# TensorE streams the identity into unused columns of the products' PSUM bank

## The chip, the cores and the metric

The kernel runs on one core of a Trainium2 chip. The metric is the device time of one execution in microseconds (us). Smaller is better.

## The reference

Attention with a top-k mask feeds a feed-forward block with squared ReLU.

```python
# q, k, v: (8, 8, 576, 64) f32; w_in: (512, 2048); w_out: (2048, 512)
scores = scale * q @ k^T                        # per batch and head, 576 x 576
kth = np.partition(scores, -32, axis=-1)[..., -32:-31]
scores = np.where(scores >= kth, scores, -1e9)  # keep each row's 32 largest
scores = scores - scores.max(-1, keepdims=True)
attn = np.exp(scores) / (np.exp(scores).sum(-1, keepdims=True) + 1e-9)
x = (attn @ v).transpose(0, 2, 1, 3).reshape(4608, 512)
h = np.maximum(x @ w_in, 0.0)
out = h * h @ w_out
```

## The kernel before

The attention is cut into 144 steps (`U = 144`). A step `u` handles two blocks of 128 rows of scores, each 576 wide. The steps are software-pipelined, and the instruction order on each engine is written out by hand (`pin` keeps it). In the main loop, while VectorE searches the 32 largest of step `u`, TensorE makes the scores of `u + 1`, and ScalarE, GpSimd and the DMA queues carry the weights of earlier steps on.

One step on the four engines, in the names of the profile:

- **Scores.** `scores(u + 1)` (L319) fills two PSUM banks, `sc_a` with the first halves of the rows and `sc_b` with the second. `sc_a` may be written once VectorE's `most` (L352) of the step before has read it. `sc_b` may be written once VectorE's two operations on `cats` (L376, L377) have read what it held. Between `sc_a` and `sc_b` TensorE does what `in_gap` holds: the ten products of an older step's weights with the values (`weigh`, L570, into the bank `av_ps`), the transposes of finished tokens (L648, L666) and of the coming pair's q and k (L202).
- **Copies.** ScalarE copies both halves to the tile `s` (L329: `s<-sc_a`, then `s<-sc_b`). Then VectorE forms `most` from `sc_a` and the copied second half.
- **Search.** VectorE runs four rounds of `MAX8` and `MATCH_REPLACE8` (L443, L445, L451). Its place for `most` of the next step is between the third and the fourth round.
- **Weights.** ScalarE makes the exponentials (L526), a DMA transposes them to `wT` (L535), `weigh` sums them with the values, VectorE inverts the row sums (L586, L591) and ScalarE's `place` scales the result into `x_tok` or `x_rem` (L610, L615).
- **Dense block.** After the scores TensorE runs pieces of the feed-forward block: `up` (L695, sixteen matmuls of 128 columns) and `down` (L765, four of 512 columns). Where no piece is ready, `idle_piece` (L786) streams the identity into the bank `dn_ps`. From step 123 on, a written table (`PLAN`) says which pieces run; in that stretch `carry_far` (L392) also moves a part of `most` back into `sc_b` on TensorE in some steps.

The bank `av_ps` holds three steps' products of 2 x 65 columns each, so 390 of its 512 columns are used.

Of the kernel before, what the change touches and what calls it, by code (L numbers as in the profile page):

```python
# [13 lines left out]
f32 = mybir.dt.float32  # L14
# [9 lines left out]
def kernel(  # L24
# [9 lines left out]
    nc = tc.nc  # L34
# [53 lines left out]

    flags = const.tile([128, 6, 8 * 4 * 9], bf16, name="flags")
    cats = const.tile([128, 2, 2, WIDE], f32, name="cats")  # L90
    av = ps_one.tile([128, 3, 2, 65], f32, name="av_ps")


    pairs = [(b, pr) for b in range(B) for pr in range(H // 2)]
# [2 lines left out]

    fetches = []
    after_far, next_far = [], []

    def by_head(t):
        return t.rearrange("p (a d) -> p a d", a=2)
# [77 lines left out]
    def prep_units(i):  # L180
        q_raw, k_raw, v_raw = raw[i]
        qkT = heads.tile([128, 512 + 640], f32, name="qkT")
        qT, kT = qkT[:, 0:512], qkT[:, 512:1152]
        k_rest = kT.rearrange("p (n d) -> p n d", d=64)[:, 0:10:9]
        bd, va = qbd[i % 5], vau[i % 8]
        prep[i] = (qT, kT, bd, va)

        def twice(t):
            return t.rearrange("p (o d) -> p o d", o=1).broadcast_to([128, 2, 64])

        def main(which, src):
            bank = []

            def turn_chunks(some):
                if not bank:
                    bank.append(ps_one.tile([128, 512], f32, name="gen", bufs=2))
                for c in some:
                    if side_by_side(i):
                        pin(nc.tensor.transpose(bank[0][:, c * 128:(c + 1) * 128], src[:, c * 128:(c + 1) * 128], id_f[:, :]))
                        continue  # L200
                    for a in range(2):
                        pin(nc.tensor.matmul(out=bank[0][64 * a:64 * a + 64, c * 128:(c + 1) * 128], lhsT=src[:, a * 256 + c * 64:a * 256 + (c + 1) * 64],  # L202
                                             rhs=id_f[:, :], start=True, stop=True))

            def go():
                turn_chunks((2, 3) if bank else range(4))
                pin(nc.scalar.activation((qT, kT[:, 64:576])[which], bank[0][:, :], AF.Copy, scale=(scale, 1.0)[which]))
                next_far.append(lambda: last_values(which))
            go.ahead = lambda: turn_chunks((0, 1))
            return go  # L210


        def first_step():
            for j, bank in ((0, "gen"), (1, "gen"), (2, "dn_ps"), (3, "sc_a")):
                if bank == "sc_a":
                    tp = ps_sc.tile([128, 2, 512], f32, name=bank)[:, 0, :]
                else:
                    tp = ps_one.tile([128, 512], f32, name=bank, bufs=2 if bank == "gen" else None)
                if j < 2:
                    for c in range(2):  # L220
                        pin(nc.tensor.transpose(tp[:, c * 128:(c + 1) * 128], k_raw[:, 2 * j + c], id_f[:, :]))
                    to, got = kT[:, 64 + j * 256:64 + (j + 1) * 256], tp[:, 0:256]
                elif j == 2:
                    pin(nc.tensor.transpose(tp[:, 0:128], q_raw[:, 0], id_f[:, :]))
                    to, got = qT[:, 0:128], tp[:, 0:128]
                else:
                    pin(nc.tensor.transpose(tp[:, 0:64], k_raw[0:64, 4], id_f[0:64, 0:64]))
                    to, got = k_rest, twice(tp[:, 0:64])
                if j % 2:
                    pin(nc.vector.tensor_copy(to, got))  # L230
                else:
                    pin(nc.scalar.activation(to, got, AF.Copy, scale=scale if j == 2 else 1.0))

        def first_q():
            tp = ps_one.tile([128, 512], f32, name="gen", bufs=2)
            for c in range(1, 4):
                pin(nc.tensor.transpose(tp[:, c * 128:(c + 1) * 128], q_raw[:, c], id_f[:, :]))
            pin(nc.scalar.activation(qT[:, 128:512], tp[:, 128:512], AF.Copy, scale=scale))

        def rest(both=(0, 1)):  # L240
            tp = ps_one.tile([128, 512], f32, name="gen", bufs=2)
            for which in both:
                src = (q_raw, k_raw)[which]
                last = src[0:64, 512:640] if i else src[0:64, 4]
                pin(nc.tensor.transpose(tp[:, which * 64:(which + 1) * 64], last, id_f[0:64, 0:64]))
            if 0 in both:
                pin(nc.scalar.activation(bd[0:64, 0:64], tp[0:64, 0:64], AF.Copy, scale=scale))
                pin(nc.scalar.activation(bd[64:128, 64:128], tp[64:128, 0:64], AF.Copy, scale=scale))
            if 1 in both:
                pin(nc.scalar.activation(k_rest, twice(tp[:, 64:128]), AF.Copy))  # L250

        def last_values(x):
            assert i < 8 or av_left[i - 8] == 0
            half = slice(64 * x, 64 * x + 64)
            pin(nc.scalar.activation(va[half, 4 + x, :, 0:64], by_head(v_raw[half, 512:640]), AF.Copy))

        def values():
            assert i < 8 or av_left[i - 8] == 0
            pin(nc.scalar.activation(va[:, 0:4, :, 0:64], v_raw[:, 0:512].rearrange("p (a c d) -> p c a d", a=2, c=4), AF.Copy))

        def all_values():
            values()
            last_values(0)
            last_values(1)

        if i == 0:
            return [first_step, first_q, all_values, lambda: rest((0,))]
        return [main(0, q_raw), main(1, k_raw), rest, values]
# [37 lines left out]
    def scores(u, between=None):  # L306
        ps = [ps_sc.tile([128, 2, 512], f32, name=f"sc_{j}") for j in "ab"]
        js = (1, 0) if u < 2 else (0, 1)

        def half(j):  # L310
            for x, (i, c, a) in enumerate(steps[u]):
                qT, kT, bd, va = prep[i]
                k0 = j * HALF + 64 * (1 - x)
                if c < 4:
                    r = slice(64 * a, 64 * a + 64)
                    lhsT, rhs = qT[r, c * 128:(c + 1) * 128], kT[r, k0:k0 + HALF]
                else:
                    lhsT, rhs = bd[:, :], kT[:, k0:k0 + HALF]
                pin(nc.tensor.matmul(out=ps[j][:, x, 0:HALF], lhsT=lhsT, rhs=rhs, start=True, stop=True))  # L319

        half(js[0])
        if not between:
            half(js[1])
        two_s = scores_of[u // 2 % 3]
        s = two_s[:, u % 2]
        st[u] = {"s": s, "ps": ps, "both_s": two_s}
        st[u]["cat"] = cats[:, u % 2]
        for j in js:
            pin(nc.scalar.activation(s[:, :, j * HALF:(j + 1) * HALF], ps[j][:, :, 0:HALF], AF.Copy, scale=sign(u)))  # L329
            if u == 0 and j == 1:  # L330
                pairs_of(0)
                soon.pop(0)()
            if between and j == js[0]:
                between()
                half(js[1])
        for i, c, a in steps[u]:
            qk_left[i] -= 1
# [291 lines left out]
    def x_unit(now, b, c):  # L629
# [12 lines left out]
        def by_tensor():  # L642
            if late:
                tp = bank(2, [128, 2 * KH, 128], bf16)[:, 0:KH]
            else:
                tp = ps_one.tile([128, KH, 128], bf16, name="gen", bufs=2)[:, :, :]
            for kh in range(KH):
                pin(nc.tensor.transpose(tp[:, kh, :], x_tok[b, c][:, kh * 128:(kh + 1) * 128], id_h[:, :]))  # L648

            def rest():  # L650
                if late:
                    pin(nc.vector.tensor_copy(to, tp))
                else:
                    pin(nc.scalar.activation(to, tp, AF.Copy))  # L654
                if late or at_step[0] >= U - 2:
                    done()
                else:
                    fresh.append(done)
            return rest
# [18 lines left out]
    def block(xt, stores):  # L678
# [3 lines left out]

        def up(f0):
            def go():
                if f0 == 0:
                    held["h2"] = ffp.tile([128, NF, 128], bf16, name="h2", bufs=5)
                if tail:
# [70 lines left out]

        def down(c, part):
            def go():  # L760
                if part == 0:
                    held["op"] = ps_one.tile([128, 512], f32, name="dn_ps")
                op = held["op"]
# [17 lines left out]
        ups.extend(up(f) for f in range(0, NF, per))  # L781

    def idle_piece():
        hp = ps_one.tile([128, 512], f32, name="dn_ps")
        for kh in range(KH):
            pin(nc.tensor.matmul(out=hp[:, :].rearrange("p (o n) -> p o n", o=4), lhsT=id_h[:, :], rhs=id_h[:, :].rearrange("p (o n) -> p o n", o=1).broadcast_to([128, 4, 128]),  # L786
# [180 lines left out]
    for u in range(U):  # L967
# [94 lines left out]
            turn_x(u)  # L1062
        if u < U - 2:
            dense(u, 1)
        load_weights(1 if u else 2)

    assert len(ups) == 2 and not downs and len(behind) == 1 and not fresh and not moves and not soon_moves
# [217 lines left out]
```

## Time and profile before

| | |
|---|---|
| median of 3 runs | 852.09 us (849.92 to 852.37) |
| profiled execution, its own time | 850.69 us |
| its span, first to last instruction | 848.9 us |
| mean granted TensorE clock | 0.982 of 2.4 GHz |
| VectorE (DVE) busy | 811.6 us, 96% |
| ScalarE (ACT) busy | 759.0 us, 89% |
| GpSimd (POOL) busy | 741.4 us, 87% |
| TensorE (PE) busy | 687.5 us, 81% |

The profile comes from one execution. A busy share is an average over the start, the long middle (about 20 to 690 us), the stretch in which `PLAN` rules (about 690 to 826 us) and the end. TensorE's matmuls overlap, so two that follow each other at full rate start closer together than one lasts. The granted clock is given as a share: 1.00 is 2.4 GHz and 0.50 is 1.2 GHz.

### The profile page before, as it was taken

The numbers are of one execution on the slowest core, as the hardware profiler recorded it, in microseconds if no ns is written. First come the engines' busy times: TensorE is split into PE (matmuls) and PEld (weight loads), VectorE is DVE, ScalarE is ACT, GpSimd is POOL, SyncE is SP. The second block draws the span as 40 slices with busy tenths as digits, with TensorE's granted clock in tenths as the row PEclk, the third lists the DMA queues.
The fourth block names the chain that finished last, engine by engine and source line by source line (L and its number), as shares of the span: only waits on it lengthen the run. The fifth ranks groups of instructions, "written<-read, shape, count | busy, mean of one in ns | idle before, by whom it ended". The sixth has DMA issues, their size and how long they took to land.

```text
span 848.9 us, 21844 instructions
## 1 busy us (share of the span) xinstructions
PE 687.5 (81%) x6901; PEld 434.4 (51%) x6992; DVE 811.6 (96%) x3697; ACT 759.0 (89%) x1699; POOL 741.4 (87%) x781
## 2 busy tenths in 40 slices
PE   7678887887788788777888778787888788888986
PEld 3334345554555555455555555555555554556555
DVE  5999999999999999999999999999999999989993
ACT  4677779999999999999999999999999999989894
POOL 8998988988889889999889989898889997988982
PEclk9999999999999999999999999999999989999999
DMA  8889999999999999999999999999999998677862
GB/s 174 161 138 212 206 206 182 200 206 228 205 203 210 214 224 200 208 212 209 227 195 201 215 213 216 206 214 215 223 199 227 226 204 194 171 155 165 184 149 56
DMA packets 247371, 166.61 MB, mean 196 GB/s; under 512 B 200016, under 2 KB 224848, under 8 KB 247248
## 3 DMA queue, kind: packets, MB, share of 16 engines
q1 hardware_dynamic: 224544, 80.32, 54.2%
q0 software_dynamic: 21488, 84.42, 41.2%
q8 instruction: 57, 0.93, 0.5%
q14 instruction: 66, 0.54, 0.2%
q10 hardware_dynamic: 1216, 0.39, 0.2%
HBM read 37.75 MB, written 9.44 MB: 56 GB/s over the span
## 4 chain that ended last, share of the span: by engine, by line
DVE 53%; ACT 21%; PE 13%; issue 6%; DMA 3%; POOL 2%; SPq 0%; ACTq 0%; POOLq 0%; DVEq 0%
DVE m L445 14%; DVE cats L451 13%; DVE cats L443 8%; DVE most L352 8%; PE sc_a L319 5%; DVE cats L445 4%; DVE cats L376 4%; ACT rl L702 3%; DVE cats L377 3%; ACT w_two_b L526 2%; ACT w_two_c L526 2%; ACT w_two_a L526 2%; ACT sc_b L383 2%; ACT s_c L329 1%; PE sc_b L319 1%
## 5 line engine op out<-in xcount | busy, mean ns | idle before, releaser
L445 DVE MAX8 m<-cats 128x8 f32<-128x116 f32 (+3 forms) x864 | 259.9, 342 | 0.0
L410 POOL TENSOR_TENSOR cats<-cats,most 128x576 int32<-128x576 int32 (+1 forms) x144 | 230.3, 1599 | 3.2 <-DVE most L352 1.0
L695 PEld LDWEIGHTS <-w_in 128*128 128x128 bf16 x2304 | 142.7, 100 | 38.7 <-issue 16.7
L451 DVE MATCH_REPLACE8 cats<-m,cats 128x116 f32<-128x116 f32 (+1 forms) x576 | 157.7, 281 | 0.0
L319 PE MATMUL sc_b<-qkT 64*128 64x288 f32 x512 | 100.4, 466 | 62.8 <-DVE cats L377 56.2
L695 PE MATMUL gen<-xT,w_in 128*128 128x128 bf16 x2016 | 136.7, 224 | 4.1 <-ACT xT L654 3.3
L765 PE MATMUL dn_ps<-w_out,h 128*128 128x512 bf16 x456 | 125.5, 389 | 12.0 <-issue 8.5
L319 PE MATMUL sc_a<-qkT 64*128 64x288 f32 x512 | 98.0, 459 | 41.5 <-DVE most L352 38.2
L443 DVE MAX8 cats<-cats 128x8 f32<-128x288 f32 (+1 forms) x288 | 113.2, 434 | 0.0
L712 ACT ACTIVATE h<-rl 128x512 bf16<-128x512 f32 x136 | 85.7, 630 | 4.3
L702 ACT ACTIVATE rl<-gen 128x512 f32<-128x512 f32 x142 | 83.5, 588 | 3.2 <-PE gen L695 2.7
L401 POOL TENSOR_TENSOR cats<-s_c 128x576 int32<-128x576 int32 (+1 forms) x48 | 66.4, 1383 | 21.0 <-ACT s_c L329 19.3
L319 PEld LDWEIGHTS sc_b<-qkT 64*128 64x128 f32 x512 | 41.6, 190 | 82.5 <-PE av_ps L570 34.1
L570 PEld LDWEIGHTS <-wT 128*128 128x128 bf16 (+1 forms) x1600 | 54.8, 100 | 56.2 <-issue 46.8
L401 POOL TENSOR_TENSOR cats<-s_a 128x576 int32<-128x576 int32 (+1 forms) x48 | 65.2, 1357 | 20.2 <-ACT s_a L329 17.1
L401 POOL TENSOR_TENSOR cats<-s_b 128x576 int32<-128x576 int32 (+1 forms) x48 | 65.2, 1358 | 17.1 <-ACT s_b L329 14.8
L319 PEld LDWEIGHTS sc_a<-qkT 64*128 64x128 f32 x512 | 40.0, 188 | 74.0 <-DVE most L352 49.2
L383 ACT ACTIVATE sc_b<-most 128x288 f32<-128x288 f32 x136 | 57.1, 420 | 22.6 <-DVE most L352 19.0
L765 PEld LDWEIGHTS <-h 128*128 128x128 bf16 x544 | 45.4, 99 | 59.3 <-issue 22.5
L451 DVE MATCH_REPLACE8 cats<-cats 128x96 f32<-128x96 f32 x288 | 67.4, 241 | 0.0
L376 DVE TENSOR_TENSOR cats<-sc_b,most 128x288 f32<-128x288 f32 x144 | 63.1, 438 | 1.7 <-ACT sc_b L383 1.7
L377 DVE TENSOR_TENSOR cats<-sc_b,most 128x288 f32<-128x288 f32 x144 | 64.2, 446 | 0.0
(243 smaller groups left out, 1682.8 us busy)
## 6 DMA issues: line engine op xcount, KB each, us to landing
s_a<-gone_b POOLq DMA_DIRECT2D x9, 1152.0 KB, 7.8
s_b<-gone_a POOLq DMA_DIRECT2D x9, 1152.0 KB, 8.0
s_c<-gone_b POOLq DMA_DIRECT2D x9, 1152.0 KB, 7.6
s_a<-gone_a POOLq DMA_DIRECT2D x9, 1152.0 KB, 7.8
s_b<-gone_b POOLq DMA_DIRECT2D x9, 1152.0 KB, 7.7
s_c<-gone_a POOLq DMA_DIRECT2D x8, 1152.0 KB, 7.8
v_raw<-in_v_dram SPq DMA_DIRECT2D x64, 128.0 KB, 3.5
k_raw<-in_k_dram SPq DMA_DIRECT2D x63, 128.0 KB, 3.5
```

Source lines behind the costliest of these rows:

```text
L319: pin(nc.tensor.matmul(out=ps[j][:, x, 0:HALF], lhsT=lhsT, rhs=rhs, start=True, stop=True))
L376: pin(tt(in_two(cat[:, :, QUADS:NEXT]), far, near, op=ALU.max))
L377: pin(tt(in_two(cat[:, :, SMALL:QUADS]), far, near, op=ALU.min))
L401: pin(tt(less, s[:, :, 0:wide].bitcast(i32), s[:, :, HALF:HALF + wide].bitcast(i32), op=ALU.add))
L410: pin(tt(less, less, d["most"][:, :, 0:wide].bitcast(i32), op=ALU.subtract))
L443: pin(nc.vector.max(out=cat[:, x, NEXT:TOPS], in_=cat[:, x, 0:searched]))
L445: pin(nc.vector.max(out=m[r][:, x, :], in_=part(r, x)))
L451: pin(nc.vector.match_replace(out=part(r, x), in_to_replace=m[r][:, x, :], in_values=part(r, x), imm_value=NEG))
L695: pin(nc.tensor.matmul(out=hp[:, n * n_rows:(n + 1) * n_rows], lhsT=w_in[:, kh, (f0 + n) * 128:(f0 + n + 1) * 128], rhs=xt(kh), start=(kh ...
L702: pin(nc.scalar.activation(kept["rl"][:, :], hp, AF.Relu))
L712: pin(nc.scalar.activation(h2, flat, AF.Square))
L765: pin(nc.tensor.matmul(out=op[:, :], lhsT=held["h2"][:, f, c * 128:(c + 1) * 128], rhs=w_out[:, f, :], start=(f == 0), stop=(f == NF - 1)))
```

## The change

The tile of the products' bank becomes all 512 columns wide; the products keep columns 0 to 389. A new function `keep_warm(n)` gives TensorE `n` matmuls that stream 122 columns of the identity into columns 390 to 511, which nothing reads. It is called in two places, from step 8 on: eight matmuls in `scores`, behind what `in_gap` holds and ahead of the second half of the scores; and up to eight at the end of a step, behind its dense pieces, if the work counted in `pe_work` (a rough sum of the step's transposes and dense pieces in us) is under 2.4.

```diff
-    av = ps_one.tile([128, 3, 2, 65], f32, name="av_ps")
+    av_bank = ps_one.tile([128, 512], f32, name="av_ps")
+    av = av_bank[:, 0:390].rearrange("p (t x d) -> p t x d", t=3, x=2)
...
+    pe_work = [0.0]
+
+    def keep_warm(n):
+        for _ in range(n):
+            pin(nc.tensor.matmul(out=av_bank[:, 390:512], lhsT=id_h[:, :], rhs=id_h[:, 0:122], start=True, stop=True))
...
             def turn_chunks(some):
...
+                pe_work[0] += 0.11 * len(some)
...
             if between and j == js[0]:
                 between()
+                if u >= 8:
+                    keep_warm(8)
                 half(js[1])
...
+            pe_work[0] += 0.3
...
+                pe_work[0] += 0.9
...
+                pe_work[0] += 0.86
...
+        pe_work[0] += 0.86
...
         if u < U - 2:
             dense(u, 1)
+            if u >= 8 and pe_work[0] < 2.4:
+                keep_warm(min(8, int((2.4 - pe_work[0]) / 0.055)))
+            pe_work[0] = 0.0
```

In the program this gives 1682 new matmuls, each with its own weight load: 136 groups of eight ahead of the second half of the scores, and 98 groups of two to eight at step ends. The order on VectorE, ScalarE, GpSimd and SyncE, and what their instructions wait for, stays as it was.

On TensorE, in the step whose scores have the number 137 (in the stretch that `PLAN` rules), the piece before ends the ten products (`av_ps<-vau_g`) and goes on to `sc_b`:

```order
L570 LDWEIGHTS wT
L570 MATMUL av_ps<-vau_g,wT 128x65
L319 MATMUL sc_b<-qkT 128x288 [waits DVE_49,PE_49]
L319 MATMUL sc_b<-qkT 128x288
L695 LDWEIGHTS w_in
```

In the changed kernel the same place (its lines are counted eight to twelve further on) reads:

```order
L580 LDWEIGHTS wT
L580 MATMUL av_ps<-vau_g,wT 128x65
L106 LDWEIGHTS id_h
L106 MATMUL av_ps<-id_h 128x122
...
L106 LDWEIGHTS id_h
L106 MATMUL av_ps<-id_h 128x122
L327 MATMUL sc_b<-qkT 128x288 [waits DVE_49,PE_49]
L327 MATMUL sc_b<-qkT 128x288
L707 LDWEIGHTS w_in
```

Eight pairs of a weight load and a matmul now stand between the last product and `sc_b`, in front of the wait of `sc_b`; they wait for nothing themselves.

On TensorE at a step end in the middle of the run (the dense piece of step 71, then the scores of 72), the piece before is:

```order
L765 LDWEIGHTS h_5841
L765 MATMUL dn_ps<-w_out,h_5841 128x512
L319 MATMUL sc_a<-qkT 128x288 [waits DVE_49]
L319 MATMUL sc_a<-qkT 128x288
L570 LDWEIGHTS wT [waits DMAHW5_49]
L570 MATMUL av_ps<-vau_g,wT 128x65 [waits Activation_49]
```

And in the changed kernel:

```order
L778 LDWEIGHTS h_6629
L778 MATMUL dn_ps<-w_out,h_6629 128x512
L106 LDWEIGHTS id_h
L106 MATMUL av_ps<-id_h 128x122 [waits Activation_49]
...
L327 MATMUL sc_a<-qkT 128x288 [waits DVE_49]
L327 MATMUL sc_a<-qkT 128x288
L580 LDWEIGHTS wT [waits DMAHW5_49]
L580 MATMUL av_ps<-vau_g,wT 128x65
```

The wait for ScalarE (for `place`, which reads the bank) has moved from the first product, behind `sc_a`, to the first new matmul, ahead of `sc_a`. That is so in 97 of the 98 groups at step ends.

## Rows read from the trace of the kernel before

**Rows 1.** Windows of the middle and the late stretch: start:end, length, busy by engine.

```profile
20.00:690.00 670.00, 541.37 (x5467) 338.21 (x5535) 665.57 (x3047) 615.50 (x1387) 602.61 (x594) 0.99 1.03 207
690.00:826.00 136.00, 117.75 (x1198) 77.35 (x1211) 125.86 (x580) 123.12 (x270) 116.25 (x117) 0.96 0.77 172
```

**Rows 2.** Timeline of a middle step, all engines: start, length, engine, line, operation [idle before].

```profile
402.20 0.76 PE L319 MATMUL sc_b<-qkT 64*128 64x288 f32 x4 [0.28 <-DVE cats L377]
...
403.86 0.64 ACT L329 ACTIVATE s_c<-sc_b 128x576 f32<-128x576 f32 x1
...
404.75 0.74 DVE L352 SCALAR_TENSOR_TENSOR most<-s_c,sc_a 128x576 f32<-128x576 f32 x1
404.87 0.53 ACT L610 ACTIVATE x_tok<-av_ps,rthree 128x64 bf16<-128x64 f32 x2
...
405.55 0.76 PE L319 MATMUL sc_a<-qkT 64*128 64x288 f32 x4 [0.18 <-DVE most L352]
```

**Rows 3.** Timeline of a late step, scores number 123, all engines.

```profile
694.22 0.76 PE L319 MATMUL sc_b<-qkT 64*128 64x288 f32 x4
...
695.02 0.65 ACT L329 ACTIVATE s_b<-sc_b 128x576 f32<-128x576 f32 x1
695.71 0.75 DVE L352 SCALAR_TENSOR_TENSOR most<-s_b,sc_a 128x576 f32<-128x576 f32 x1 [0.21 <-ACT s_b L329]
```

**Rows 4.** The same two ends of a late step, scores number 142.

```profile
811.74 0.76 PE L319 MATMUL sc_b<-qkT 64*128 64x288 f32 x4
...
813.23 0.76 DVE L350 TENSOR_TENSOR most<-sc_a,s_c 128x576 f32<-128x576 f32 x1
```

**Rows 5.** The same two of scores number 136.

```profile
776.08 0.76 PE L319 MATMUL sc_b<-qkT 64*128 64x288 f32 x4
...
777.70 0.76 DVE L352 SCALAR_TENSOR_TENSOR most<-s_c,sc_a 128x576 f32<-128x576 f32 x1 [0.34 <-ACT s_c L329]
```

**Rows 6.** The same two in a middle step, scores number 40.

```profile
232.44 0.65 PE L319 MATMUL sc_b<-qkT,qbd_e 128*128 128x288 f32 x2
...
233.81 0.75 DVE L352 SCALAR_TENSOR_TENSOR most<-s_c,sc_a 128x576 f32<-128x576 f32 x1
```

**Rows 7.** TensorE's timeline, up pieces and waits, 742 to 830 us.

```profile
752.14 0.76 PE L392 MATMUL sc_b<-most,id_f 128*128 128x144 f32 x4 [1.97 <-DVE most L352]
...
754.00 1.91 PE L695 MATMUL gen<-xT,w_in 128*128 128x128 bf16 x16
...
764.23 1.95 PE L695 MATMUL gen<-xT,w_in 128*128 128x128 bf16 x32
...
769.21 1.06 PE L695 MATMUL gen<-xT,w_in 128*128 128x128 bf16 x16
```

**Rows 8.** TensorE's timeline, 686 to 732 us.

```profile
693.60 0.46 PE L570 MATMUL av_ps<-vau_b,wT 128*128 128x65 bf16 x10 [1.85 <-DVE m L445]
...
718.17 0.48 PE L570 MATMUL av_ps<-vau_c,wT 128*128 128x65 bf16 x10 [1.37 <-DMA wT<-w_two_b]
...
719.21 1.33 PE L319 MATMUL sc_b<-qkT 64*128 64x288 f32 x4
```

**Rows 9.** Windows, columns as in rows 1; the eighth figure is the granted clock.

```profile
319.70:323.10 3.40, 3.06 (x14) 1.53 (x16) 3.40 (x19) 3.16 (x8) 3.13 (x4) 0.50 1.09 281
...
695.20:698.60 3.40, 3.30 (x32) 2.92 (x30) 2.36 (x9) 2.35 (x7) 2.84 (x3) 0.50 0.30 68
719.00:722.40 3.40, 3.40 (x27) 2.11 (x22) 2.92 (x15) 2.21 (x6) 2.42 (x3) 0.51 0.92 227
753.20:756.60 3.40, 3.40 (x23) 2.40 (x21) 2.56 (x15) 2.23 (x5) 3.21 (x5) 0.50 0.76 187
```

**Rows 10.** ScalarE's timeline, 688 to 706 us.

```profile
696.72 0.60 ACT L207 ACTIVATE qkT<-gen 128x512 f32<-128x512 f32 x1 [1.05 <-PE gen L202]
```

**Rows 11.** All engines, 755 to 758 us.

```profile
757.40 0.17 DVE L591 RECIPROCAL rsum<-av_ps 128x2 f32<-128x2 f32 x1 [1.64 <-PE av_ps L570]
```

**Rows 12.** ScalarE's waits from 20 to 690 us: total us, times, longest.

```profile
ACT sc_b L383 <- DVE most L352: 18.0, 47, 0.8
```

## The prediction

> **What bounds the kernel now.** I read the windows first, to see which engine is full in which stretch. From 20 to 690 us VectorE is busy 665.6 of 670.0 us [rows 1]: it stands still for 4.4 us in all, and a change on TensorE can win no more than that there. From 690 to 826 us it is busy 125.9 of 136.0 [rows 1]: 10 us of standing still, and TensorE, at 117.8 busy, is the engine to look at.
>
> The timeline then shows how far TensorE's scores are ahead of their use. In a middle step `sc_b` ends at 402.20 + 0.76 = 402.96; ScalarE comes to copy it only at 403.86, and the copy ends 0.25 us before `most` starts at 404.75 [rows 2]. So `sc_b` has 0.90 us until ScalarE comes, and VectorE another 0.25: a delay of half a us would not reach VectorE. In a late step it is otherwise: `sc_b` ends at 694.98, the copy starts 0.04 later, `most` starts 0.04 after the copy, and VectorE has waited for it [rows 3]. From the end of `sc_b` to `most` this takes 0.73 us, the copy and two hand-overs. At 811.74 it is 0.73 again [rows 4]. Stepping through the late stretch I find nine of its 21 steps like this, at 694.2, 702.6, 719.2, 726.4, 757.3, 763.2, 782.1, 787.9 and 811.7 (rows 3 are the first, rows 4 the last). There every delay of `sc_b` is a delay of VectorE.
>
> The last view is the clock. Its mean over the run is 0.982, and the loss sits in eight short stretches at 0.50, which is 1.2 GHz; four are in the middle, four from 681 us on. In the one at 319.7 VectorE is busy for all 3.40 us: half speed on TensorE costs nothing there. In the three at 695.2, 719.0 and 753.2 it is busy 2.36, 2.92 and 2.56 us [rows 9].
>
> **What the change adds: the matmuls.** Nothing is removed. In the timeline 32 matmuls of 128 columns take 1.95 us and 16 take 1.06 [rows 7], so one more costs 0.89 / 16 = 0.056 us; one of 122 columns costs about that. Eight are 0.45 us. At half clock 16 take 1.91 [rows 7], another 0.053 each, and eight are 0.87. All 1682 are 94 us of TensorE time, which has room only where TensorE waits.
>
> **Ahead of `sc_b`.** All 136 groups stand behind the products and in front of the wait of `sc_b`. Where TensorE waits for VectorE there by more than 0.45 us, the group is free. I went through the 136 places, taking the gap between TensorE's last work and `sc_b`: 59 of them are shorter than the group. What that costs goes by the slack behind `sc_b`.
> - The nine tight late steps pay in full: 9 x 0.45 = 4.05. The one at 719.2 is at half clock [rows 9], which adds 0.87 - 0.45 = 0.42. Together 4.5.
> - Four more late steps have a little slack. At 776.08 `sc_b` ends at 776.84 and `most` starts 0.86 later, 0.13 more than the tight 0.73 [rows 5]; this step pays 0.32. The other three have between 0.14 and 0.45. Together 0.9.
> - In the middle only three steps are as tight. The one at 232.44 ends at 233.09 with `most` 0.72 later [rows 6], so it and its twin at 431 pay 0.45 each, and one at 648 pays 0.3. Together 1.2.
>
> These delays add up, since each late step's chain starts from the `most` of the step before: TensorE waits for `most` at 752.14 [rows 7], then does its dense piece, `sc_a`, the products and `sc_b` in a row.
>
> **At step ends.** Of the 98 groups, 97 now wait for ScalarE's `place` ahead of `sc_a`. In the step of rows 2 `x_tok` ends at 405.40; four matmuls then end at 405.63, where `sc_a` had started at 405.55 [rows 2]. So `sc_a` comes about 0.1 us later; over the groups I find 0 to 0.6. What is queued behind it is `sc_a` and the products, and whoever waits for those has more than a us. It counts only where `sc_b` is pushed in turn, in two steps near 325 and 331: 0.6 us together, as an estimate.
>
> That it waits at all is what the Trainium skill says against the change (PSUM — Partial Sum Buffer, "PSUM bank collisions raise a hardware error"): a matmul and a reader are to be kept apart by bank and quadrant, and other columns of the bank don't help. By that rule the free columns spare no wait; the order of the changed kernel agrees, with 97 waits, and the sum without them would be 0.6 lower.
>
> **What the clock gives back.** The three late stretches cost VectorE at most the following. At 695.2 ScalarE waits 1.05 us for transposes at half clock [rows 10]; half of it goes at full clock, 0.5. At 719.21 `sc_b` takes 1.33 instead of 0.76 [rows 3, 8], 0.6, and what follows some 0.4 more. At 753.2 VectorE waits 1.64 us for the products [rows 11] behind sixteen matmuls that took 1.91 for 1.06: 1.6 with the others there. Together 3.1 us, and nothing in the middle. But what TensorE did before each fall was to wait: 1.85 us ahead of the products at 693.60, 1.37 us for a transposed `wT` at 718.17 [rows 8], 1.97 us for `most` at 752.14 [rows 7]. The new groups stand behind the first two of these waits in the queue, and ahead of the third only by a step, so they don't fill them. I count one of the three: 1.0 us. Bounds: 0 and 3.1.
>
> The Trainium skill (TensorE: Matmul & The Clock Gate, "Why this matters for your kernels") has the opposite rule: keep TensorE busy between its bursts, and the throttle stays away. The falls behind waits agree with it; by it the credit would be 3.1 instead of 1.0.
>
> **The sum.** 4.5 + 0.9 + 1.2 + 0.6 - 1.0 = 6.2 us slower. The profiled execution took 850.7 us, 1.4 below the median of the three runs; the four lie around 851.3. Added to the first this is 856.9, to the middle of the four 857.5. I say 857.0.
>
> **The unknown in the middle.** `sc_b` comes later in 48 of the 114 middle steps in which ScalarE would already be there, so ScalarE would stand still some 14 us more there (my estimate, 0.3 us each). ScalarE is busy 615.5 of 670 [rows 1], and 18.0 us of its rest are waits for `most` [rows 12], which shrink as it gets later. That cover takes in all 14, if it lies in the right steps. If a third of it doesn't, VectorE waits up to 5 us more. Between 0 and 5 I take 0, because the middle step of rows 2 has 0.25 us for VectorE on top.
>
> **Rivals.**
> 1. *The clock pays (faster).* All three late stretches go, and the groups lie in time that TensorE would have waited. Then 851.3 - 3.1 = 848.2. For it: the clock of the late stretch, 0.96 [rows 1], and that falls follow waits. Against it: the groups cost 0.45 us in nine steps where TensorE waits for nothing. It decides from the point at which a group delays the tight steps by less than 0.2 us on average. Chance 0.09.
> 2. *No change.* The delays are real but vanish at later waits for something else: the wait of 1.37 us for a `wT` [rows 8] shows that a DMA can end last. Half of the 5.4 late us lost that way, the middle costs absorbed too and two clock stretches gone: 851.3 + 2.7 - 2 = 852. That also covers the case in which the clock stays as it is and the groups are hidden. Chance 0.24.
> 3. *ScalarE becomes the bound of the middle.* The cover of 18.0 us doesn't fit, and the waits for `place` hold TensorE up when ScalarE is late. 857 + 5 = 862. For it: ScalarE's load; against: the slack of most middle steps. Chance 0.15.
>
> The forecast keeps 0.52.
>
> **How the numbers follow.** A measurement of this kernel tells a change from none at about 0.3%, 2.6 us. Slower by more than that are the forecast and rival 3, 0.67; the same is rival 2, 0.24; faster is rival 1, 0.09. The range reaches from below the no-change case, 850.5, to rival 3 with a us on top, 863; the forecast's own range is 854 to 860.
>
> **What would show it.** In the profile after: 1682 rows of the new line, some 0.056 us apart; a granted clock nearer to 1, but with stretches at 0.50 left behind the waits for `wT` and `most`. In the middle the same 5.5 us per step and VectorE as full as before. From 690 us on, `sc_b` some 0.45 us later behind the products in the tight steps, ScalarE's copy straight behind it, and VectorE's standing still grown from 10 to about 15 us. The prediction is wrong if the stretch from 690 to 826 us gets no longer, or if the middle does.

## The result and the profile after

The change takes 861.82 us in the median (six executions, 858.13 to 864.54) against 852.23 for the piece before (849.92 to 853.73): a ratio of 1.0113, 95% interval 1.0085 to 1.0141. It is slower by some 9.6 us. The profiled execution, 858.13 us with a span of 856.3, is the fastest of the six; its own loss is 7.4 us of span.

The page of the change, its busy times and the group of the new line (busy time and mean ns of one; idle time just before, by releaser):

```profile
PE 778.9 (91%) x8674; PEld 517.1 (60%) x8674; DVE 812.9 (95%) x3697; ACT 760.8 (89%) x1699; POOL 741.6 (87%) x781
...
L106 PE MATMUL av_ps<-id_h 128*128 128x122 bf16 x1682 | 128.6, 217 | 12.9 <-ACT x_tok L620 8.8
```

TensorE's busy time is 91 us above that of before, for 94 expected, but the two pages don't compare cleanly: the one before has 6901 matmuls for 6992 weight loads, so 91 records are missing from it (88 of them of `dn_ps`), and the one after lacks none. By the timelines below eight new matmuls put the next one off by 0.44 to 0.52 us, which makes 93 to 109 us for the 1682 (an estimate). VectorE does the same work; what grew is its standing still. The windows of the change, columns as in [rows 1]; the second is the stretch that was 690 to 826 before, shifted by the 6.24 and 7.83 us by which VectorE's `most` is late at its two ends:

```profile
20.00:690.00 670.00, 620.59 (x6950) 410.67 (x6949) 660.34 (x3020) 611.23 (x1375) 597.41 (x588) 1.00 1.02 205
696.24:833.83 137.59, 124.52 (x1412) 84.21 (x1410) 126.12 (x580) 123.35 (x269) 115.90 (x117) 1.00 0.77 169
701.00:704.40 3.40, 3.40 (x54) 2.68 (x53) 2.10 (x8) 2.26 (x4) 0.74 (x1) 1.00 0.27 60
725.00:728.40 3.40, 3.40 (x49) 2.52 (x50) 3.40 (x19) 3.37 (x7) 3.21 (x4) 1.00 0.77 193
758.00:761.40 3.40, 2.64 (x26) 2.04 (x28) 3.40 (x15) 3.37 (x9) 3.40 (x4) 1.00 0.39 95
```

In the middle VectorE stands still for 670.0 - 660.3 = 9.7 us, 4.4 before [rows 1]. In the late stretch it is 137.6 - 126.1 = 11.5, 10.1 before. And the last three rows, at the places of the half-clock stretches of [rows 9], show full speed: nothing is left at 0.50 but a piece of the end.

So the loss is where the prediction had least of it. VectorE's waits in the middle name its cause (total us, times, longest):

```profile
DVE rthree L596 <- PE av_ps L106: 5.4, 9, 1.4
DVE most L362 <- ACT s_b L337: 2.6, 5, 1.1
DVE most L362 <- ACT s_c L337: 0.8, 1, 0.8
```

The first row is new. `rthree` is VectorE's reciprocal of the row sums, which reads the bank `av_ps`. It now waits for the new matmuls, though these write other columns. The waits for copies are 3.4 us in all; before they were 4.1 (0.3 of it for `s_a`):

```profile
DVE most L352 <- ACT s_b L329: 2.7, 5, 1.2
DVE most L352 <- ACT s_c L329: 1.1, 2, 0.9
```

The timeline around one of the nine places, scores number 40, that of [rows 6]; in the piece before:

```profile
230.09 0.47 PE L570 MATMUL av_ps<-vau_h,wT 128*128 128x65 bf16 x10
...
231.69 0.19 DVE L586 RECIPROCAL rthree<-av_ps 128x6 f32<-128x6 f32 x1
```

and in the change:

```profile
231.13 0.47 PE L580 MATMUL av_ps<-vau_h,wT 128*128 128x65 bf16 x10
...
231.44 0.39 PE L659 MATMUL gen<-id_h,x_tok 128*128 128x128 bf16 x4
...
231.75 0.66 PE L210 MATMUL gen<-id_f,k_raw 128*64 128x128 f32 x8
...
232.34 0.60 PE L106 MATMUL av_ps<-id_h 128*128 128x122 bf16 x8
...
232.98 0.20 DVE L596 RECIPROCAL rthree<-av_ps 128x6 f32<-128x6 f32 x1 [0.77 <-PE av_ps L106]
```

The products, whose sums the reciprocal wants, end at 231.13 + 0.47 = 231.60. Before, they ended at 230.56 and the reciprocal came 1.1 us after, so it had that in hand. Now it runs at 232.98, straight after the eight matmuls end at 232.94. Between products and eight stand twelve transposes, so the reciprocal waits for those too: 1.34 us beyond the products, of which only 0.6 are the new matmuls. In eight of the nine places four to twelve transposes stand there; at steps 115 and 118 they wait in turn for ScalarE, 0.60 and 0.76 us.

The ninth place, step 120, has none. There a group at a step end waits for `place`, and the scores and the products come behind it:

```profile
680.82 0.32 PE L106 MATMUL av_ps<-id_h 128*128 128x122 bf16 x3 [0.88 <-ACT x_tok L620]
681.07 0.76 PE L327 MATMUL sc_a<-qkT 64*128 64x288 f32 x4
681.76 0.48 PE L580 MATMUL av_ps<-vau_b,wT 128*128 128x65 bf16 x10
```

`place` ends at 680.77. The products start 0.99 us after it; in the piece before they start 0.05 us after it, at 675.59, and `sc_a` runs at 674.59, while `place` is still awaited.

The late step of [rows 4] in the change:

```profile
818.36 0.48 PE L580 MATMUL av_ps<-vau_f,wT 128*128 128x65 bf16 x10
...
818.68 0.59 PE L106 MATMUL av_ps<-id_h 128*128 128x122 bf16 x8
...
819.20 0.76 PE L327 MATMUL sc_b<-qkT 64*128 64x288 f32 x4
819.37 0.17 DVE L601 RECIPROCAL rsum<-av_ps 128x2 f32<-128x2 f32 x1 [0.53 <-PE av_ps L106]
...
820.68 0.76 DVE L360 TENSOR_TENSOR most<-sc_a,s_c 128x576 f32<-128x576 f32 x1
```

From `sc_b` to `most` it is 0.72 us behind the end (820.68 - 819.96), the tight 0.73 of before; `sc_b` itself is 0.43 further behind the products. The reciprocal runs 1.01 us behind the start of the products, 0.59 before: late by as much, so two paths delay this step equally.

### The profile page after: what moved, and what is told of

It reads as the page before. It is cut to its first block, busy times and chain, and to the rows that moved or that the text cites. A ratio compares the mean times of both kernels' runs of the same rounds, so it can differ in the third digit from the quotient of the medians.

```text
span 856.3 us, 25293 instructions
## 1 busy us (share of the span) xinstructions
PE 778.9 (91%) x8674; PEld 517.1 (60%) x8674; DVE 812.9 (95%) x3697; ACT 760.8 (89%) x1699; POOL 741.6 (87%) x781
## 4 chain that ended last, share of the span: by engine, by line
DVE 45%; ACT 26%; PE 17%; issue 6%; DMA 2%; POOL 2%; SPq 0%; ACTq 0%; POOLq 0%; DVEq 0%
DVE cats L461 12%; DVE m L455 11%; DVE cats L453 7%; DVE most L362 6%; PE sc_a L327 4%; ACT rl L714 3%; DVE cats L455 3%; DVE cats L386 3%; PE sc_b L327 3%; PE av_ps L106 2%; ACT w_two_b L536 2%; ACT w_two_c L536 2%; ACT w_two_a L536 2%; PE dn_ps L778 2%; PE gen L210 2%
## 5 line engine op out<-in xcount | busy, mean ns | idle before, releaser
L707 PEld LDWEIGHTS <-w_in 128*128 128x128 bf16 x2304 | 137.4, 98 | 33.7 <-issue 10.7
L106 PE MATMUL av_ps<-id_h 128*128 128x122 bf16 x1682 | 128.6, 217 | 12.9 <-ACT x_tok L620 8.8
L778 PE MATMUL dn_ps<-w_out,h 128*128 128x512 bf16 x544 | 138.6, 381 | 1.3 <-ACT wide L786 1.3
L707 PE MATMUL gen<-xT,w_in 128*128 128x128 bf16 x2016 | 131.6, 219 | 2.0 <-ACT xT L665 0.9
L106 PEld LDWEIGHTS <-id_h 128*128 128x128 bf16 x1682 | 99.1, 98 | 32.0 <-issue 24.9
L327 PE MATMUL sc_b<-qkT 64*128 64x288 f32 x512 | 97.9, 457 | 21.4 <-DVE cats L387 14.3
```

What stands on the lines that cost most here:

```text
L106: pin(nc.tensor.matmul(out=av_bank[:, 390:512], lhsT=id_h[:, :], rhs=id_h[:, 0:122], start=True, stop=True))
L707: pin(nc.tensor.matmul(out=hp[:, n * n_rows:(n + 1) * n_rows], lhsT=w_in[:, kh, (f0 + n) * 128:(f0 + n + 1) * 128], rhs=xt(kh), start=(kh ...
L778: pin(nc.tensor.matmul(out=op[:, :], lhsT=held["h2"][:, f, c * 128:(c + 1) * 128], rhs=w_out[:, f, :], start=(f == 0), stop=(f == NF - 1)))
```

## The experiments

Two theories. **R** (A in the last expectations): what costs is that a reader of the bank has to wait for the new matmuls and all that stands ahead of them. **P** (B): what costs is TensorE's time ahead of `sc_b`, as the prediction had it. An end group is one at the end of a step. The table follows VectorE: the start of `most` of a step in each profile, less its start before, in us.

| kernel | 119 | 122 | 123 | 126 | 128 | 133 | 143 |
|---|---|---|---|---|---|---|---|
| the change | 5.2 | 6.2 | 7.9 | 8.1 | 6.5 | 5.4 | 7.8 |
| e10, the change again | 5.4 | 6.5 | 9.5 | 9.8 | 8.2 | 6.9 | 9.2 |
| e11, without one end group | 5.4 | 6.4 | 6.8 | 7.0 | 8.0 | 6.8 | 9.1 |
| e2, no end groups | 5.9 | 6.0 | 7.8 | 8.0 | 7.1 | 6.4 | 8.7 |
| e4, one matmul, no end groups | 5.2 | 5.2 | 5.2 | 5.6 | 5.1 | 5.1 | 6.0 |
| e1, other bank | 8.3 | 9.2 | 12.1 | 12.5 | 11.6 | 10.4 | 13.7 |
| e5, behind the products | 1.3 | 4.0 | 8.1 | 7.8 | 6.2 | 5.0 | 7.5 |
| e7, the same, no end groups | 0.3 | 0.4 | 2.1 | 2.0 | 1.0 | 0.4 | 2.7 |
| e8, from scores 123 on | 1.6 | 1.6 | 2.3 | 3.4 | 2.1 | 0.9 | 3.2 |
| e3, only end groups | 0.6 | 1.2 | 3.4 | 3.3 | 1.7 | 1.2 | 0.9 |
| e9, the same without that of 121 | 0.2 | 1.7 | 2.0 | 2.2 | 0.7 | 0.6 | 0.6 |
| e6, four groups by hand | 1.4 | 1.4 | 2.4 | 2.1 | 0.6 | -1.2 | -1.6 |
| e12, five groups by hand | 0.8 | 0.8 | 0.8 | 0.2 | -1.4 | -3.3 | -3.6 |

e6, e8 and e12 add nothing before step 122 and are still 0.8 to 1.6 us late there: so much does one profile vary by itself, and smaller differences are read step by step only.

**The same eight matmuls, in another bank (e1).** They go into the unused columns of the bank of `sc_a`, at the same place on TensorE. The order of the other engines and the end groups stay as in the change, for which `in_gap` hands its last piece back (`later`).

```diff
+        if between:
+            later = between()
+            if u >= 8:
+                keep_warm(8, ps[js[0]][:, 0, 390:512])
...
-                between()
-                if u >= 8:
-                    keep_warm(8)
+                if later:
+                    later()
```

Expected:

> The eight matmuls ahead of sc_b write unused columns of sc_a's bank and not of the products' bank; their number, length and place on TensorE, and the groups at step ends, stay. Theory P (the cost is TensorE's time ahead of sc_b, which makes the second copy and most late): no gain, 858 to 862 us, ratio 1.007 to 1.013. Theory R (the cost is VectorE's reciprocal, which reads the products' bank and so waits for its last writer, the eight matmuls and what stands between): the reciprocals' waits for them, 11.3 us in the profile of the changed kernel, are gone; what is left are the tight late steps (at most 5.4 us) less the clock's credit (at most 3.1): 852 to 855 us.

Measured: 863.76 us, ratio 1.0144 (1.0105 to 1.0183), no faster than the change and above what either theory expected. In its waits of the middle the reciprocal's is nearly gone, and others stand in its place:

```profile
ACT s_a L341 <- PE sc_a L106: 9.9, 11, 1.6
ACT s_c L341 <- PE sc_a L106: 8.9, 11, 1.8
ACT s_b L341 <- PE sc_a L106: 7.7, 10, 1.9
DVE most L365 <- ACT s_b L341: 6.3, 7, 2.1
...
DVE rthree L599 <- PE av_ps L583: 0.6, 1, 0.6
```

ScalarE's copy of `sc_a` reads the bank that now takes the matmuls, waits 26.5 us for them, and hands its lateness to `most`, whose waits for the three copies add up to 10.8 us (3.4 in the change). In the form "the reciprocal is to blame" R fell here. In a wider form it stands: the wait goes with the bank, to whoever reads it next.

**One matmul instead of eight (e4).** Groups of one, none at step ends.

```diff
-                    keep_warm(8)
+                    keep_warm(1)
...
-            if u >= 8 and pe_work[0] < 2.4:
-                keep_warm(min(8, int((2.4 - pe_work[0]) / 0.055)))
```

Expected:

> One matmul instead of eight ahead of sc_b, none at step ends, still in the products' bank. Theory P: an eighth of the cost, 0.056 us in some thirteen tight steps: 852 to 853 us. Theory R: the reciprocal still waits for this one matmul behind the transposes that stand ahead of it, so only some 0.4 us of each of its 17 waits goes and the rest, about 5 us, stays; no credit from the clock: 856 to 858 us.

Measured: 854.87 us, ratio 1.0038 (1.0020 to 1.0056), between the two expectations. An eighth of the matmuls ahead of `sc_b`, and the wait is still there:

```profile
DVE rthree L596 <- PE av_ps L106: 2.5, 4, 1.0
```

At the four places, steps 40, 76, 115 and 118, VectorE loses 1.2, 0.4, 0.8 and 0.5 us; a further 1.8 at step 87 is ScalarE's wait for a load and belongs to none of this. In the late tight steps, where eight cost 0.43, one costs less than 0.1. So there it is the number that counts (P), and in the middle mostly the place behind the transposes (R).

**Eight straight behind the products (e5, e7).** Same bank, same 136 places ahead of `sc_b`, but ahead of the transposes. e7 also has no end groups.

```diff
     def in_gap(u):
         products(to_weigh(u))
+        if u >= 7:
+            keep_warm(8)
...
                 between()
-                if u >= 8:
-                    keep_warm(8)
```

Expected of e5 and e7:

> The eight matmuls stand straight behind the ten products and ahead of the transposes; bank and number as in the change, step ends too. Theory P: the same work stands ahead of sc_b, 858 to 862 us. Theory R: a reciprocal waits for the eight matmuls alone, 0.45 us at most, and no longer for the transposes: its waits fall from 11.3 to some 5 us, and the time to 854 to 857.

> Eight matmuls straight behind the products, ahead of the transposes; no groups at step ends. Theory P+R (in the middle the cost is the reciprocal's wait for the transposes and the matmuls, late it is TensorE's time ahead of sc_b, and the rest is the wait for place at the end of step 121): the middle up to step 119 is about 1 us longer than before as in e5_behind, step 123 no longer jumps by 4 us, the late tight steps add 2.4: 853 to 855 us, less up to 2.8 if the clock stays full late. Theory P alone: 857 or more, as only 0.6 us of the forecast came from the step ends.

Measured: e5 856.53 us, 1.0069 (1.0042 to 1.0097); e7 854.58 us, 1.0039 (1.0019 to 1.0058). In e7 VectorE has no wait for the new line in the middle. The place of scores number 40 there:

```profile
230.43 0.59 PE L106 MATMUL av_ps<-id_h 128*128 128x122 bf16 x8
...
231.31 0.66 PE L210 MATMUL gen<-id_f,k_raw 128*64 128x128 f32 x8
231.72 0.19 DVE L594 RECIPROCAL rthree<-av_ps 128x6 f32<-128x6 f32 x1
```

The reciprocal starts while the transposes still run, 0.03 later than before, and the middle is 0.4 us late at step 122. The late steps pay 0.3 to 0.43 as in the change (steps 134 and 136 to 138). P alone would have left the middle's loss where it was, since `sc_b` has the same eight ahead of it. Most of what e7 still loses is 1.6 us at step 123: 0.43 for the group, and a half-clock stretch from 694.3 us on. e5, with end groups, is 1.3 late at 119 but jumps by 2.4 at step 120 and 4.0 at 123. At both a new matmul at a step end stands in a wait for `place`, 1.75 and 2.76 us long, and what follows runs at half clock; at 120 `place` itself is late, behind a load for which ScalarE waited 0.93 us. What end groups do there, the next runs show.

**The parts apart (e2, e3, e8).** e2 leaves out the end groups, by the last two lines of the edit of e4. e3 leaves out the groups ahead of `sc_b` instead:

```diff
-                if u >= 8:
-                    keep_warm(8)
```

e8 is e2 with groups from scores 123 on alone:

```diff
-                if u >= 8:
+                if u >= 123:
```

Expected:

> The change without its groups at step ends; the groups of eight ahead of the second half of the scores stay. Theory A (a group delays the next reader of the products' bank, the reciprocal, in the steps where transposes and group end after VectorE is there): the middle costs nearly what it cost in the change, most of step 119 starts 4.0 to 5.2 us later than before, standing of the reciprocals behind the new line is 4 us or more in the middle; the late tight steps pay 0.3 to 0.43 each; the clock gives back 2.3 to 2.8; in all 856 to 858.5. Theory B (a delay counts only through the second half of the scores, as in the prediction): most of step 119 starts at most 1.5 us later and the whole is 853 to 855.

> Only the 98 groups at step ends, none ahead of sc_b. Theory P: they push sc_b in two steps, 0.6 us; if they bring the clock to full speed, up to 3.1 us come back: 849.5 to 853 us. Theory R: the same, since the reciprocal stands ahead of these groups in program order and does not wait for them. Above 855 both are wrong about the step ends, and the 8.8 us that TensorE waits for x_tok there count.

> Eight matmuls ahead of sc_b as in the change, but only for the scores from number 123 on; none at step ends. The middle stays as before. The late tight steps add 0.3 to 0.43 us each in seven places, 2.4 to 2.8 us, and the clock gives 0 to 2.8 back: 851 to 854 us. My prediction's 5.4 us of late cost without credit would be 856.5.

Measured: e2 859.70 us, 1.0100 (1.0063 to 1.0136); e3 853.15 us, 1.0030 (1.0011 to 1.0049); e8 853.33 us, 1.0030 (1.0016 to 1.0044). The groups ahead of `sc_b` carry nearly the whole loss, and those of the middle carry most of it: e2 less e8 is 0.7% of 851, some 6 us. e2 comes out 1.2 us above the upper end of what A expected and far above B's. Its reciprocal waits 4.3 us in seven places of the middle; step 120 is not among them, and there it is only 0.07 us late, where e3, with end groups alone, is 0.6 late and the change 1.0. So of the nine places of the change one belongs mostly to an end group. Against e7, e2 has the same matmuls, the transposes on their other side, and is 0.6% slower.

e3's largest loss is 2.2 us at step 123. There a new matmul at the end of step 121 waits for `place`, and `sc_a` and the products stand behind it. ScalarE and then TensorE in the change, each from its timeline:

```profile
698.90 0.91 ACT L620 ACTIVATE x_tok<-av_ps,rthree 128x64 bf16<-128x64 f32 x4
```

```profile
699.86 0.59 PE L106 MATMUL av_ps<-id_h 128*128 128x122 bf16 x8 [2.91 <-DVE m L455]
700.38 0.76 PE L327 MATMUL sc_a<-qkT 64*128 64x288 f32 x4
701.07 0.48 PE L580 MATMUL av_ps<-vau_b,wT 128*128 128x65 bf16 x10
```

`place` (`x_tok`) ends at 699.81 and the group starts at 699.86. (The releaser that the row names, VectorE's `m`, had long been done.) The products, which always waited for this `place`, now stand behind the group (0.52) and `sc_a` (0.69) as well, and start 1.26 us after it.

**Without that one group (e9 from e3, e11 from the change).**

```diff
-            if u >= 8 and pe_work[0] < 2.4:
+            if u >= 8 and u != 121 and pe_work[0] < 2.4:
```

Expected:

> Only the groups at step ends, and none at the end of step 121, where the group waits for the place of the extra products. If that one wait is what the step ends cost (2.2 us at step 123 in e3_only_ends), the jump goes and the clock's credit at steps 127 and 128 stays: 849 to 851 us. If the step ends cost in many places, 852 to 853 as e3_only_ends.

> The change without the one end group of step 121, whose first matmul waited for place ahead of the scores of 122 and held the products of step 123 up. Theory: the jump at step 123 falls from 1.7 us in the change to 0.5 or less, and the whole is 1.0 to 1.5 us shorter than the change in the same comparison (859 to 861 if the change takes 861). Rival: the jump is chance (the landing of a transposed wT) and stays within 0.3 us of the change's.

Measured: e9 852.56 us, 1.0018 (1.0003 to 1.0033), in the range of its rival (852 to 853): its jump at step 123 is down from 2.2 us to 0.3, but its end group at step 120, where `place` was late behind a load, cost 1.5 us for 0.6 in e3, so its time doesn't show the gain; e11 859.76 us, 1.0112 (1.0075 to 1.0148), against 861.14 for the change in the same comparison. The profile of e11, ScalarE and TensorE:

```profile
699.05 0.91 ACT L620 ACTIVATE x_tok<-av_ps,rthree 128x64 bf16<-128x64 f32 x4
```

```profile
697.03 0.76 PE L327 MATMUL sc_a<-qkT 64*128 64x288 f32 x4
700.02 0.46 PE L580 MATMUL av_ps<-vau_b,wT 128*128 128x65 bf16 x10 [2.23 <-DVE m L455]
```

`sc_a` runs inside the wait again, the products start 0.06 us after `place` (699.96), and the jump at step 123 is 0.44 instead of 1.7, which is the price of the eight ahead of `sc_b`. The 1.2 us of the end group are shown at this step; in the medians the 1.4 us lie inside the intervals. At step 127 e11 then lost 1.0 to a half-clock stretch at 725.7.

**The change once more (e10).** The same kernel, for a second profile.

Expected:

> The change as it is, once more. Theory A: as in its first profile the reciprocal stands some 5 to 6 us behind the new line in the middle, most of step 119 starts 5 us later than before, late tight steps pay 0.43 each; 858 to 863. If the other executions of the change, 860 to 864, differ from the profiled one by a part of the program rather than by chance, most of step 143 starts 9 us or more later than before and one stretch holds the difference. Theory B: the middle's loss in the first profile was chance, and step 119 is at most 2 us later here.

Measured: 861.14 us, ratio 1.0130 (1.0092 to 1.0168). Up to step 122 the table's two rows agree to 0.3 us, and the reciprocals stand 5.5 us in nine places again: the loss of the middle is no chance. The two part at step 123, 3.1 us against 1.7. There TensorE fell to half clock behind the same wait for `place`:

```profile
700.05 0.59 PE L106 MATMUL av_ps<-id_h 128*128 128x122 bf16 x8 [2.91 <-DVE m L455]
...
702.21 1.02 PE L106 MATMUL av_ps<-id_h 128*128 128x122 bf16 x8
703.16 1.33 PE L327 MATMUL sc_b<-qkT 64*128 64x288 f32 x4
```

Eight matmuls put `sc_b` off by 0.95 us here, for 0.52 in the first profile, and `sc_b` takes 1.33 for 0.76. The jump is 0.43 for the group, 1.2 for the end group and 1.4 for this stretch. The same sum gives e2 (0.43 + 1.4 = 1.8, no end group) and, nearly, e3 (1.2 + 1.0). So the first profile of the change, without one such stretch, shows it at its best. The other executions had a mean clock of 0.992 to 0.996 against its 0.999; that their 2 to 6 us more come from there is likely, but they left no trace.

**A few matmuls where TensorE waits (e6, e12).** Nothing of the change is kept but `keep_warm`. e6 has four groups: 12 at the end of step 125, 16 ahead of the products of step 126, and 12 ahead of the moved part of `most` in steps 131 and 134, these last into unused columns of the bank of `sc_b`, which TensorE itself writes next. e12 adds 16 ahead of the products of step 122.

```diff
+        if u == 122:
+            keep_warm(16, st[u + 1]["ps"][1][:, 0, 390:512])
+        if u == 126:
+            keep_warm(16)
...
+        if u in (131, 134):
+            keep_warm(12, st[u + 1]["ps"][1][:, 0, 390:512])
...
+            if u == 125:
+                keep_warm(12)
```

Expected:

> New matmuls only in four places where TensorE waited before: 12 at the end of step 125, 16 ahead of the products of step 126 (which waited 1.37 us for wT), 12 each ahead of the carried copy of most in steps 131 and 134 (into unused columns of sc_b's bank). If the clock's credit is as large as the profile of the changed kernel shows (0.55 + 1.03 + 1.18 = 2.8 us around steps 127, 128 and 133) and these places bring it without the costs: 848 to 849 us, ratio 0.996 to 0.998. If filling these waits doesn't lift the clock, 851 to 852.

> The kernel with the few matmuls set by hand in four waits, and sixteen more ahead of the products of step 122, where TensorE waited 1.85 us before the half-clock stretch at 695. If the wait is what the fall follows, that stretch is gone and ScalarE gets its transposed tokens 0.5 us sooner: 848.5 to 849.0. Rival: the stretch stays or nothing there ends last, 849.0 to 849.6, the same as with four groups. If the sixteen delay the products, 849.6 to 850.

Measured: e6 849.19 us against 851.00, ratio 0.9981 (0.9965 to 0.9997); e12 850.23 us against 850.82, ratio 0.9991 (0.9974 to 1.0009). TensorE in e6, where the stretches at 719.0 and 753.2 were:

```profile
717.61 0.80 PE L106 MATMUL av_ps<-id_h 128*128 128x122 bf16 x12 [0.42 <-ACT x_tok L618]
718.34 0.76 PE L327 MATMUL sc_a<-qkT 64*128 64x288 f32 x4
719.03 1.03 PE L106 MATMUL av_ps<-id_h 128*128 128x122 bf16 x16
719.89 0.47 PE L578 MATMUL av_ps<-vau_c,wT 128*128 128x65 bf16 x10
```

```profile
751.74 0.80 PE L106 MATMUL sc_b<-id_h 128*128 128x122 bf16 x12 [1.18 <-ACT s_a L337]
752.54 0.76 PE L400 MATMUL sc_b<-most,id_f 128*128 128x144 f32 x4
...
753.99 1.06 PE L705 MATMUL gen<-xT,w_in 128*128 128x128 bf16 x16
```

The matmuls lie in waits, both stretches are gone, and VectorE gains 0.56, 1.02 and 1.61 us at steps 127, 128 and 133, together 3.2. The first of these is not shown to be the clock's. e4 has it too, 0.56 us at step 127, though its clock fell there (from 724.0 us on) and `sc_b` took 1.33 us; what had shrunk was the wait for the `wT`, from 1.37 us [rows 8] to 0.51:

```profile
722.89 0.48 PE L580 MATMUL av_ps<-vau_c,wT 128*128 128x65 bf16 x10 [0.51 <-DMA wT<-w_two_b]
...
724.05 1.33 PE L327 MATMUL sc_b<-qkT 64*128 64x288 f32 x4
```

In e12 the stretch at 695 goes too and VectorE gains another 0.67 at step 124. At step 143 e12 is 3.6 us ahead of the piece before, but its span is only 1.8 shorter (847.1 to 848.9). The chain that ended last shows where the rest went: start, length and row, in the piece before, e6 and e12 in this order:

```profile
815.71 4.07 DMA wT<-w_two_b
```

```profile
814.03 4.72 DMA wT<-w_two_b
```

```profile
811.95 5.94 DMA wT<-w_two_b
```

The transposed weights for the last steps were wanted 3.8 us sooner in e12 than before and landed only 1.9 sooner (817.89 to 819.78). A credit beyond that is lost at this DMA, in these three profiles. So the four groups are worth at most some 0.2%: e6 gains 1.8 us in the median and e12, which has the same four and a fifth, 0.6, with an interval that takes in no change at all. e6 came out just above what it expected, e12 above all three of its ranges.

## Why the prediction came out as it did

The direction held: slower, and 861.8 lies inside the range, near its upper end, though above the forecast's own 854 to 860. The 857.0 was 4.8 us short. Against the profiled execution, on whose time the sum was made, it was short by 1.2; the terms behind it were further off.

**The middle is the step that failed.** The prediction wrote 'What that costs goes by the slack behind `sc_b`', found three tight steps, and gave the middle 1.2 us, with 0.6 for the step ends. The profile has 6.2 at step 122. Increments of 0.3, 0.8, 0.3, 0.8, 0.3, 0.4, 1.1, 0.9 and 1.0 at steps 22, 40, 58, 76, 94, 112, 115, 118 and 120 make 5.9 of it, and each has a wait of the reciprocal behind the new line (the last by way of an end group). Only three of the nine were among its tight steps, and these cost twice to four times the forecast. It followed `sc_b` to its consumers and did not ask who else reads the bank that the matmuls write. It used the rule of the bank, for `place` at the step ends, and stopped there. That the order of VectorE and the semaphores it waits on 'stays as it was' did not show that one of those waits now ends later. e7 took the transposes out of this wait and with them the loss; e4 kept them and kept half of it; e1 moved the bank and the wait moved along. The Trainium skill (PSUM — Partial Sum Buffer, "PSUM bank collisions raise a hardware error") asks to guard a bank and quadrant, not an address; the 5.4 us of `rthree` agree: unused columns are no free place.

**The late stretch** was over-sized. The price was right: a group costs 0.43 for the 0.45 forecast. Six of the nine tight steps paid it (123, 133, 134, 137, 138, 142), 2.6 us for 4.5. Step 124 paid too: its `sc_b` starts 1.12 us behind the start of the transposes ahead of it in the change and 0.59 in e12, 0.53 for the group; it is hidden by a gain there, below. Steps 127 and 128 show no charge, as the change gains there what e3 gains without such groups. Of the four partial ones, 136 paid 0.30 (forecast 0.32) and 143 paid 0.37; 139 and 140 nothing; step 126, not on the list, 0.28. In all some 4.0 for 5.4. Whether `sc_b` or the reciprocal ends last there stays open: both are late by the same amount, and e1, where this reciprocal doesn't wait for the group, still pays 0.3 to 0.7 a step.

**The clock** was under-sized: -1.03 and -1.18 at steps 128 and 133, the second with 0.43 of charge in it, are 2.6 for the 1.0 counted. Step 124 adds 0.67, by e12, which gains that there without the group; the 0.55 of step 127 is not shown to be the clock's (e4). Together 3.9 with it, 3.3 without, so the upper bound of 3.1 was nearly the truth. The reason for counting one of three, that the groups don't lie in the waits, fell: the wait for `most` ahead of the stretch at 753 is still 1.67 us in the change (1.97 before) and the clock held; ahead of the one at 719 the wait for the `wT` is gone from the change's timeline, with 0.34 us for `place` in its place. Of the signs, VectorE's standing still in the late stretch grew to 11.5 us and not to 15, and no stretch at 0.50 was left behind the waits. The end groups alone cleared the stretch at 719 and not that at 753 (e3, e9); the groups ahead of `sc_b` cleared both (e7, e8). By the Trainium skill (TensorE: Matmul & The Clock Gate, "Why this matters for your kernels"), TensorE kept busy between its bursts keeps its clock; the trace agrees in sum, but not place by place: behind a wait of 2.91 us the clock held in one profile of the change and fell in the other.

**Step ends**: 0.6 forecast at two places near 325 and 331, where nothing of that size shows. The cost lies at step 120, 0.6 by e3 (more where a load is late, 1.5 in e9), and at step 123, 1.2. The prediction allowed that `sc_a` and the products queue behind the new wait, 'and whoever waits for those has more than a us'; at these two steps nobody has, since `sc_a` used to run inside the wait for `place` and now runs after it.

**Rival 3** named 862, nearly the time measured, by a mechanism that did not occur: `most` waits for ScalarE's copies no longer than before in the middle. Rival 1's credit came in full and was outweighed. Of rival 2's delays that 'vanish at later waits' there are the two late steps without a charge.

The falsifier that the prediction set itself, 'or if the middle does', came true. That the sum held is owed to errors of both signs: +4.4 in the middle, -1.4 (charges) and -2.9 (gains) in the late stretch, +1.2 at step 123. The sum was luck, and the step of it that failed is the middle's.

## What to carry to other kernels

Work put into unused columns of a bank is work for every reader of that bank: list its next readers, and put the new matmuls straight behind the last one that they wait for anyway, not behind other work. Price filler by place: the same eight matmuls cost 5 us less on the other side of the transposes, and 52 matmuls in chosen waits gave at most some 0.2% where 1682 took 1.1%. A group that must wait for a reader takes the work behind it out of that wait, as at steps 120 and 123; putting it behind what can run meanwhile was not tried here. And a mean clock is no gain by itself: it was 0.999 in the slower kernel and 0.985 in the fastest.

## What was not expected of the hardware

Half clock did not come back at the same places. The piece before had eight stretches ahead of the end, e6 seven, and those of e6 before 690 us lie elsewhere, with the same program there. One place is nearly constant, the wait ahead of the products of step 123, 1.85 us in the piece before and 2.22 to 2.91 in the other profiles: the clock fell around its end in eleven of thirteen profiles and held in two, the first profile of the change (2.91 us of waiting) and e11 (2.23). In e12, where sixteen matmuls left 1.11 us of the wait, it held. What set the two apart is open: e10 and e2 waited 2.91 and 2.22 us and fell.

The price hangs on what the stretch covers. In the piece before it began at 695.2, just behind `sc_b` of step 123. In e6 it began at 694.7, ahead of the products, `sc_b` took 1.33 us for 0.76, and the step cost 1.0 us more. In e4 it began again behind `sc_b`, at 700.1, and the step cost 0.06. So behind this wait a fall was likely, but its price can't be forecast from the wait; only from where it falls.
